# Transposing unit 4's x with the DMA crossbar in place of the tensor engine

## The chip, the core and the metric

The kernel runs on one core of one Trainium2 chip. The metric is device time in microseconds (us) of one execution, start to end; less is better. Engines are named as the profile names them: PE is the tensor engine and PEld its weight loads, DVE the vector engine, ACT the scalar engine, POOL and SP two further ones that issue DMAs. A DMA *lands* when its last data have arrived; times to landing are counted from its issue. A profiled execution also has a *span*, from its first to its last recorded instruction, and every timed run lists its span too. The time of the kernel before is 1.73 to 1.91 us longer than its span in all of its listed runs.

## The reference

Chunked attention (8 batches, 8 heads, 576 tokens, head size 64, chunks of 64), whose output, 4608 tokens by 512, goes through a two-layer network with a gated activation:

```python
scores = scale * q_c @ k_c.T                  # per chunk of 64
attn   = softmax(scores)
x      = (attn @ v_c)  ->  (B*S, H*D) = (4608, 512)
h = x @ w_in                                  # 512 -> 2048
g = h * (1 / (1 + exp(-beta * h)))
out = g @ w_out                               # 2048 -> 512
```

## The kernel before

The tokens are cut into 18 units of 256. Two units form a block of 512 tokens, on which the network runs. For each unit: the scores (`emit_sc`), the product with v (`emit_pv`), a division by the sum that leaves x in fp16 (`emit_norm`), and a transpose of x, since the first layer needs its features on the partitions. Each unit has two halves of 128 tokens. The transpose comes in two kinds:

```python
def emit_xt_pe(u, s, copy=nc.scalar.copy):          # on the tensor engine
    xf = x16_t.pop((u, s)).rearrange("p r h d -> p (r h d)")
    ...
    for g in range(4):
        nc.tensor.transpose(out=xp[:, g, :], in_=xf[:, g * 128:(g + 1) * 128], identity=ident)
    copy(out=xt_at(u, s), in_=xp)                   # PSUM -> SBUF, on ACT

def emit_xt_dma(u, s):                              # in the DMA crossbar
    xf = x16_t.pop((u, s)).rearrange("p r h d -> p (r h d)")
    nc.sync.dma_start_transpose(out=xt_at(u, s), in_=xf)
```

`emit_T` transposes a unit's keys and queries: on DVE (by blocks) for units below 8, by DMA from SP from unit 8 on. The network of block j is `emit_m(j, m)`, first layer, which reads the transposed x; and `emit_t(j, t, k0, k1)`, second layer, ending in an output DMA from SP. The second layer of one block is spread among the first layer of the next. The program order is written by hand; the part that matters:

```python
        emit_t(1, 0, 0, 8)
        emit_pv(4)
        emit_norm(4, 0)
        emit_norm(4, 1)
        emit_T(5)
        emit_T(6)
        emit_t(1, 0, 8)
        emit_xt_pe(4, 0)
        emit_xt_pe(4, 1)
        emit_t(1, 1, 0, 8)
        emit_sc(5)
        emit_t(1, 1, 8)
        ...                                   # unit 5 in the same way, on the tensor engine
        for m in range(KFF):                  # block 2 = units 4 and 5
            emit_m(2, m)
            ...                               # units 6 and 7: emit_norm, emit_xt_dma
        for j in range(3, NB):                # block 3 = units 6 and 7, and so on
            items = [(0.02 + 0.98 * m / KFF, 0, ("m", m)) for m in range(KFF)]
            for t in range(4):
                for hf in range(2):
                    items.append((0.98 * (t + 0.5 * hf) / 4, 1, ("t", t, hf)))
            ...                               # attention items of the next two units
            items.sort(key=lambda it: it[:2]) # so t(j-1, 0, first half) is ahead of m(j, 0)
```

So eight matmuls of the old block stand ahead of the new block's first matmul.

The softmax here doesn't subtract the row's maximum and nothing guards it: scores larger than these inputs give would overflow.

Of the kernel before, what the change touches and what calls it, by code (L numbers as in the profile page):

```python
# [15 lines left out]
def kernel(  # L16
# [108 lines left out]
    def loads_to(u):  # L125
        while nxt[0] <= min(u, NU - 1):
            load_unit(nxt[0])
            nxt[0] += 1
# [16 lines left out]
    def emit_T(u, which=("kT", "qT")):  # L145
        for nm in which:
            src, dst = {"kT": (k_t, kT), "qT": (q_t, qT)}[nm]
            a = src.pop(u)
            t = qt_p.tile([128, H, CH, 2], FP16, tag=nm, name=nm)
            dst[u] = t  # L150
            if u >= XU:
                nc.sync.dma_start_transpose(
                    out=t.rearrange("p h s e -> p (h s e)").rearrange("p (j t) -> p j t", t=128),
                    in_=a.rearrange("p h r d -> p (h r d)"),
                )
                continue
            nc.vector.transpose(
                out=t.rearrange("p h s e -> p (h s e)").bitcast(FP32).rearrange(
                    "p (h i r) -> p h r i", h=H, r=2),
                in_=a.rearrange("p h r d -> p (h r d)").bitcast(FP32).rearrange(  # L160
                    "p (h r i) -> p h r i", h=H, r=2),
            )
        if which[-1] == "qT" and u not in (6, 7, 8):
            loads_to(u + 4)
# [89 lines left out]
    def emit_pv(u, where=("x", "s")):  # L254
        et = et_t.pop(u)
        for s in (1, 0) if u >= MU else (0, 1):
            i = 2 * u + s
            if where[s] == "p":
                x = [ps_p.tile([128, 4, 128], FP32, tag="p", name=f"y{r}") for r in range(2)]
            else:  # L260
                pool = {"x": ps_x, "s": ps_s}[where[s]]
                x = [pool.tile([128, 2, 4, 128], FP32, tag=where[s], name="x")]
            for g in range(4):
                for r in range(2):
                    for c in range(2):
                        nc.tensor.matmul(  # L266
                            out=(x[0][64 * c:64 * c + 64, r, g, 0:D + 1] if len(x) == 1 else
                                 x[r][64 * c:64 * c + 64, g, 0:D + 1]),
                            lhsT=(et[64 * r:64 * r + 64, s, 4 * c + g, :] if u < XU else
                                  et[64 * r:64 * r + 64, g % 2, 4 * s + 2 * c + g // 2, :]),  # L270
                            rhs=vbig[64 * r:64 * r + 64, i, 4 * c + g, 0:D + 1],
                        )
            x_t[u, s] = x
# [6 lines left out]
    def emit_norm(u, s):  # L280
        x = x_t.pop((u, s))
        rd = rd_p.tile([128, 2, 4, 1], FP32, tag="rd", name="rd")
        x16 = x_p.tile([128, 2, 4, D], FP16, tag="x16", name="x16")
        for r, z in [(slice(0, 2), x[0])] if len(x) == 1 else list(enumerate(x)):
            nc.vector.reciprocal(out=rd[:, r], in_=z[..., D:D + 1])  # L285
            o = x16[:, r]
            nc.vector.tensor_tensor(  # L287
                out=o, in0=z[..., 0:D], in1=rd[:, r].to_broadcast(list(o.shape)), op=ALU.mult
            )
        x16_t[u, s] = x16  # L290

    def xt_at(u, s):
        j, o = unit_block[u]
        if j not in xt_t:
            xt_t[j] = xt_p.tile([128, 4, 4, 128], FP16, tag="xt", name="xt")
        return xt_t[j][:, 2 * o + s]

    def emit_xt_pe(u, s, copy=nc.scalar.copy):
        xf = x16_t.pop((u, s)).rearrange("p r h d -> p (r h d)")
        tag = "s" if u < 2 and (u, s) != (1, 0) else "xp"[s]  # L300
        xp = {"x": ps_x, "s": ps_s, "p": ps_p}[tag].tile([128, 4, 128], FP16, tag=tag, name="xp")
        for g in range(4):
            nc.tensor.transpose(out=xp[:, g, :], in_=xf[:, g * 128:(g + 1) * 128], identity=ident)  # L303
        copy(out=xt_at(u, s), in_=xp)  # L304
# [11 lines left out]
    def emit_xt_dma(u, s):  # L316
        xf = x16_t.pop((u, s)).rearrange("p r h d -> p (r h d)")
        nc.sync.dma_start_transpose(out=xt_at(u, s), in_=xf)
# [36 lines left out]
    def emit_t(j, t, k0=0, k1=None):  # L355
        k1 = KFF if k1 is None else k1
        if k0 == 0:
            ops_t[j, t] = ps_p.tile([128, DM], FP32, tag="p", name="ops")
        ops = ops_t[j, t]
        for kk in range(k0, k1):  # L360
            nc.tensor.matmul(  # L361
                out=ops,
                lhsT=gt_t[j][:, kk, t * 128:(t + 1) * 128],
                rhs=w_out16[kk // 4][:, kk % 4, :],
                start=(kk == 0),
                stop=(kk == KFF - 1),
            )
        if k1 < KFF:
            return
        osb = osb_p.tile([128, DM], FP32, tag="osb", name="osb")  # L370
        nc.scalar.activation(out=osb, in_=ops, func=ACTF.Copy, scale=0.5)  # L371
        r0 = blocks[j][0] * UNIT + t * 128
        nc.sync.dma_start(out=out[r0:r0 + 128, :], in_=osb)
# [20 lines left out]
    with tc.manual_schedule():  # L394
# [111 lines left out]
                emit_ex(4)  # L506
        emit_t(1, 0, 0, 8)
        emit_pv(4)
        emit_norm(4, 0)
        emit_norm(4, 1)  # L510
        emit_T(5)
        emit_T(6)
        emit_t(1, 0, 8)
        emit_xt_pe(4, 0)
        emit_xt_pe(4, 1)
        emit_t(1, 1, 0, 8)
        emit_sc(5)
        emit_t(1, 1, 8)
# [125 lines left out]
```

## Time and profile before

| | kernel before |
|---|---|
| time, first three runs | 288.05 us median (287.95 to 288.5) |
| profiled span | 286.6 us |
| tensor engine (PE) busy | 98% of the span, 96% of the chain of waits |
| PE waits after 58 us | none |
| transposes of x: on PE (four per half unit) / by crossbar (one per half unit) | 48 (40 at line 303, 8 at line 311) / 24 |

The view of groups: line, engine, operation, output from inputs, shape, count; then busy us, mean ns of one; then idle time before, by releaser.

```profile
L303 PE MATMUL xp<-ident,x 128*128 128x128 f16 x40 | 3.5, 219 | 0.1
```

The transposes of unit 7's x, asked for by their line between 90.2 and 92 us, of which the second, issued at 91.2, landed after 4.1 us, at 95.3:

```profile
DMA to landing us min/median/max: 4.1/4.4/4.7
```

And the waits of SP's queue in the last microseconds (us in total, times, longest): line 639 is the end of the program, where SP waits for outstanding DMAs.

```profile
SPq L639 <- DMA out_dram<-osb: 1.3, 3, 0.5
```

### The profile page before, as it was taken

What the parts mean: (1) busy time and instruction counts of PE and PEld (TensorE: products, weight loads), DVE (VectorE), ACT (ScalarE), POOL (GpSimd) and SP (SyncE); (2) the same over time, 40 slices, a digit from 0 to 9 for tenths busy, and PEclk for the clock granted to TensorE, in tenths of its full rate; (3) what the DMA queues carried; (4) which work ended last, traced back from release to release, by engine and by line L of the source; (5) the groups of instructions that cost most, each with busy time, mean ns of one, the idle gap of its engine ahead of it and who ended that gap; (6) DMA issues with size and microseconds to landing.
All of it is one profiled execution on the core that took longest, in us unless ns stands there. A gap on an engine that the chain in (4) does not pass through costs nothing.

```text
span 286.6 us, 6655 instructions
## 1 busy us (share of the span) xinstructions
PE 280.4 (98%) x2777; PEld 136.4 (48%) x2777; DVE 141.9 (49%) x260; ACT 147.0 (51%) x225; POOL 95.7 (33%) x125
## 2 busy tenths in 40 slices
PE   6989999999999999999999999999999999999995
PEld 3564456545544444444444444444444444444444
DVE  2778444776567544534454445454554545333300
ACT  3478228774557545454545454554545444444411
POOL 8853678487172992070907160000000000000000
PEclk9999999999999999999999999999999999999999
DMA  8999999999999999999999999565451212010012
GB/s 193 175 196 206 182 180 215 206 166 165 153 95 182 155 176 167 165 119 168 137 158 145 143 124 171 129 75 128 57 129 39 73 39 73 37 39 37 37 73 75
DMA packets 139997, 37.14 MB, mean 130 GB/s; under 512 B 126912, under 2 KB 135488, under 8 KB 139968
## 3 DMA queue, kind: packets, MB, share of 16 engines
q0 software_dynamic: 99136, 17.83, 82.4%
q1 hardware_dynamic: 40688, 18.83, 32.2%
q8 instruction: 22, 0.36, 0.5%
q14 instruction: 7, 0.06, 0.1%
q10 hardware_dynamic: 144, 0.07, 0.1%
HBM read 36.71 MB, written 9.44 MB: 161 GB/s over the span
## 4 chain that ended last, share of the span: by engine, by line
PE 96%; ACT 1%; POOL 1%; issue 1%; DVE 0%; DVEq 0%; POOLq 0%
PE hps L329 44%; PE ops L361 43%; PE warm L381 2%; PE x L266 2%; PE sc L238 1%; PE sc L225 1%; PE ops L600 1%; ACT xt L304 1%; PE xp L303 1%; POOL h L401 1%; PE sc L198 1%; POOL vbig L113 1%; ACT et L208 0%; PE y L266 0%; PE xp L311 0%
## 5 line engine op out<-in xcount | busy, mean ns | idle before, releaser
L343 DVE SCALAR_TENSOR_TENSOR gt<-sg,hps 128x512 f16<-128x512 f32 (+1 forms) x153 | 99.1, 654 | 107.4 <-ACT sg L339 107.2
L339 ACT ACTIVATE sg<-hps,beta 128x512 f32<-128x512 f32 (+1 forms) x153 | 100.4, 663 | 72.9 <-PE hps L329 72.8
L329 PE MATMUL hps<-xt,win 128*128 128x512 f16 (+1 forms) x612 | 136.8, 367 | 0.8 <-ACT xt L304 0.7
L361 PE MATMUL ops<-wout,gt 128*128 128x512 f16 x560 | 131.2, 379 | 0.0
L329 PEld LDWEIGHTS <-win 128*128 128x128 f16 x612 | 58.1, 98 | 62.1 <-issue 1.0
L361 PEld LDWEIGHTS <-gt 128*128 128x128 f16 x560 | 53.9, 98 | 63.4
L371 ACT ACTIVATE osb<-ops 128x512 f32<-128x512 f32 x35 | 20.9, 598 | 42.5 <-PE ops L361 42.5
L113 POOL DMA_DIRECT2D vbig<-in_v_dram x40 | 34.1, 871 | 9.6 <-DMA wout<-in_moe_w_out_dram 3.7
L99 POOL DMA_DIRECT2D qu<-in_q_dram x22 | 18.7, 863 | 40.1 <-DMA qT<-qu 37.1
L287 DVE TENSOR_TENSOR x<-x,rd 128x512 f16<-128x512 f32 x31 | 21.4, 691 | 1.2
L99 POOL DMA_DIRECT2D ku<-in_k_dram x22 | 18.9, 877 | 0.6 <-DMA ku<-in_k_dram 0.6
L285 DVE RECIPROCAL rd<-x 128x8 f32<-128x8 f32 x31 | 6.2, 200 | 12.0 <-PE x L266 12.0
L247 ACT ACTIVATE et<-sc 128x1024 f16<-128x1024 f32 (+1 forms) x8 | 6.4, 811 | 8.2 <-PE sc L238 8.2
L231 ACT ACTIVATE et<-sc 128x1024 f16<-128x1024 f32 x10 | 10.2, 1018 | 0.2
L266 PEld LDWEIGHTS <-et 64*64 64x64 f16 x576 | 6.0, 107 | 7.3 <-issue 3.8
L381 PE MATMUL warm<-idle 128*128 128x512 f16 x22 | 8.2, 518 | 0.0
L105 POOL DMA_DIRECT2D ku<-in_k_dram x9 | 6.8, 756 | 2.5 <-DMA win<-in_moe_w_in_dram 1.3
L266 PE MATMUL x<-vbig,et 64*64 64x65 f16 x496 | 7.3, 194 | 0.2 <-ACT et L208 0.2
L105 POOL DMA_DIRECT2D qu<-in_q_dram x9 | 6.8, 767 | 1.4 <-DMA win<-in_moe_w_in_dram 0.7
L612 DVE TENSOR_SCALAR osb<-ops 128x256 f32<-128x256 f32 (+1 forms) x2 | 0.7, 357 | 12.1 <-PE ops L600 12.1
L131 POOL DMA_DIRECT2D win<-in_moe_w_in_dram x8 | 6.0, 757 | 1.2 <-DMA vbig<-in_v_dram 0.9
L304 ACT COPY xt<-xp 128x512 f16<-128x512 f16 x9 | 5.1, 588 | 2.3 <-PE xp L303 2.2
(46 smaller groups left out, 73.4 us busy)
## 6 DMA issues: line engine op xcount, KB each, us to landing
out_dram<-osb SPq DMA_DIRECT2D x35, 256.0 KB, 3.7
vbig<-in_v_dram POOLq DMA_DIRECT2D x32, 128.0 KB, 7.6
qu<-in_q_dram POOLq DMA_DIRECT2D x20, 128.0 KB, 4.9
ku<-in_k_dram POOLq DMA_DIRECT2D x20, 128.0 KB, 6.8
win<-in_moe_w_in_dram POOLq DMA_DIRECT2D x8, 256.0 KB, 9.0
wout<-in_moe_w_out_dram POOLq DMA_DIRECT2D x4, 512.0 KB, 12.3
qu<-in_q_dram POOLq DMA_DIRECT2D x3, 256.0 KB, 7.7
ku<-in_k_dram POOLq DMA_DIRECT2D x3, 256.0 KB, 8.0
```

The source lines that it names most:

```text
L99: nc.gpsimd.dma_start(out=tv[off:off + n, sp], in_=src[b, :, s:s + n, :].rearrange("h p d -> p h d"),)
L105: nc.gpsimd.dma_start(out=t[off // 2:(off + n) // 2], in_=src[b, :, s:s + n, :].rearrange("h (p r) d -> p h r d", r=2),)
L113: nc.gpsimd.dma_start(out=vbig[off:off + n, i, :, 0:D], in_=v[b, :, s:s + n, :].rearrange("h p d -> p h d"),)
L231: nc.scalar.activation(out=et, in_=sc, func=ACTF.Exp, scale=scale)
L266: nc.tensor.matmul(out=(x[0][64 * c:64 * c + 64, r, g, 0:D + 1] if len(x) == 1 else x[r][64 * c:64 * c + 64, g, 0:D + 1]), lhsT=(et[64 * r ...
L287: nc.vector.tensor_tensor(out=o, in0=z[..., 0:D], in1=rd[:, r].to_broadcast(list(o.shape)), op=ALU.mult)
L329: nc.tensor.matmul(out=hps[:, 0:n], lhsT=w_in16[m // 2][:, kk, (m % 2) * 128:(m % 2) * 128 + 128], rhs=xr[:, c0 // CH:(c0 + n) // CH, 2 * ...
L339: nc.scalar.activation(out=sg[:, 0:n], in_=hps[:, 0:n], func=ACTF.Tanh, scale=beta2[:, m:m + 1])
L343: nc.vector.scalar_tensor_tensor(out=gt_t[j][:, m, c0:c0 + n], in0=sg[:, 0:n], scalar=1.0, in1=hps[:, 0:n], op0=ALU.add, op1=ALU.mult,)
L361: nc.tensor.matmul(out=ops, lhsT=gt_t[j][:, kk, t * 128:(t + 1) * 128], rhs=w_out16[kk // 4][:, kk % 4, :], start=(kk == 0), stop=(kk == K ...
L371: nc.scalar.activation(out=osb, in_=ops, func=ACTF.Copy, scale=0.5)
L381: nc.tensor.matmul(out=d[:, 0:w], lhsT=idle[:, 0:128], rhs=idle[:, 0:w])
```

## The change

The intent is to relieve the tensor engine, which sets the time: its transposes of unit 4's x go to the crossbar. The second half is normalized first so that its transfer starts early, and unit 5's block transposes on DVE run between the two norms. Unit 5's x stays on the tensor engine.

```diff
         emit_t(1, 0, 0, 8)
         emit_pv(4)
+        emit_norm(4, 1)
+        emit_xt_dma(4, 1)
+        emit_T(5)
         emit_norm(4, 0)
-        emit_norm(4, 1)
-        emit_T(5)
+        emit_xt_dma(4, 0)
         emit_T(6)
         emit_t(1, 0, 8)
-        emit_xt_pe(4, 0)
-        emit_xt_pe(4, 1)
         emit_t(1, 1, 0, 8)
```

## The prediction

> **What bounds the kernel now.** I read the page first: busy shares, the 40 slices, the chain that ended last.
>
> ```profile
> PE 280.4 (98%) x2777; PEld 136.4 (48%) x2777; DVE 141.9 (49%) x260; ACT 147.0 (51%) x225; POOL 95.7 (33%) x125
> ...
> PE   6989999999999999999999999999999999999995
> ...
> DMA  8999999999999999999999999565451212010012
> ...
> PE 96%; ACT 1%; POOL 1%; issue 1%; DVE 0%; DVEq 0%; POOLq 0%
> ```
>
> The tensor engine is busy in every slice after the first few, and 96% of the chain is its own work. The other compute engines are about half idle, so their time is worth something only where PE waits for it. The DMA engines are full until about slice 26 (near 186 us), so a transfer added early has to share.
>
> The chain of waits, cut to the stretch where the change lies (start us, us, what):
>
> ```profile
> 63.91 0.38 PE x L266 x32
> 64.29 1.83 PE ops L361 x8
> 66.12 0.45 PE xp L303 x8
> 66.57 1.73 PE ops L361 x8
> 68.30 0.64 PE sc L238 x64
> 68.94 1.83 PE ops L361 x8
> 70.77 0.38 PE x L266 x32
> 71.14 1.83 PE ops L361 x8
> 72.98 0.45 PE xp L303 x8
> 73.42 0.64 PE sc L238 x64
> 74.06 1.83 PE ops L361 x8
> 75.90 0.86 PE hps L329 x4
> ```
>
> Each start is the previous start plus its length: nothing on PE waits here. The `xp` piece at 66.12 is the eight transposes that the change removes; the one at 72.98 is unit 5's and stays. The view of waits, asked for PE between 58 and 100 us, lists none at all; the PE waits of the whole run (at most 1.2 us each) lie before that.
>
> **What the Trainium skill says.** "TensorE: Matmul & The Clock Gate", Part 4, says a PE transpose ends in PSUM, so a copy has to follow, and puts one at about 275 ns in a kernel's context. Here one record lasts 219 ns, but they are pipelined: eight take 0.45 us of the chain, 56 ns each, and I use that. "Advanced Engine Details and Errata", X-Bar Transpose, says transposing DMAs are as fast as regular ones. The trace agrees when the engines are idle: 128 x 512 fp16 (128 KB) landed 2.5 us after issue at 79.1 us. "DMA: Bandwidth & Descriptors", Queues, rings and completion order, says each DMA engine goes round the queues packet by packet, so a transpose is not stuck behind the whole load backlog but shares with it. The trace agrees in kind: outputs on the hardware queue landed in 3.7 and 5.2 us in the crowded 66 to 77 us. The same page, Silent corruption, warns of two transposing streams; all transposes here are issued from SP, one stream, so I expect a correct result.
>
> **The change, part by part.**
>
> Removed from PE: eight transposes and their weight loads, 0.45 us of the chain. What follows them is the same 8-matmul group; in the list it takes 1.73 us after a transpose and after another full matmul group, 1.83 us only after the small attention matmuls. After the change its predecessor is a full matmul group, so it stays at 1.73. Net on PE: -0.45 us.
>
> Removed from ACT: two PSUM copies, 1.07 us together. ACT then reaches exp(5) with no copies ahead. But PE did not wait for that exp: pv(5) came at 70.70 and exp had ended at 69.00 + 1.02 = 70.02, behind eight covering matmuls. Worth 0.
>
> Removed from PSUM: one use of each of two pools. The next users wait for an older tile instead of a newer one; looser, and no wait was there. Worth 0.
>
> Moved on DVE: the same eight instructions in another order. From the timeline one norm takes about 0.93 us and one pair of block transposes about 1.3. The tiles of pv(4) are complete at 64.29, so norm(4,1) runs 64.3 to 65.2, unit 5's block transposes to 66.5, norm(4,0) to 67.4, unit 6's to 68.7. sc(5) will be reached at 68.30 - 0.45 = 67.85. Its keys and queries are ready at 66.5 (before: about 67.2), and its PSUM slot, read last by norm(4,1), is free at 65.2. pv(5) at about 70.3 needs the slot freed by norm(4,0) at 67.4. No new wait.
>
> Added on SP: two transposes, about 1.2 us of issue each, the first at about 65.3, the second at about 67.4. The first output of block 1 sits behind them in the same queue, so it goes out near 68.7 instead of 66.78: 1.9 us late. The instruction order shows the output buffer's next user four outputs later, so nobody should notice.
>
> Added to the DMA engines: two transposes beside the loads of units 8 and 9. The windows view (PE and so on, last three: clock, DMA share, GB/s):
>
> ```profile
> 64.00:66.00 2.00, 2.00 (x41) 1.01 (x34) 1.71 (x5) 0.00 (x0) 1.99 (x3) 1.00 2.39 152
> 66.00:68.00 2.00, 2.00 (x17) 1.09 (x15) 2.00 (x4) 1.56 (x3) 0.50 (x1) 1.00 2.39 156
> ...
> 76.00:78.00 2.00, 2.00 (x41) 0.94 (x40) 0.48 (x1) 1.22 (x2) 0.00 (x0) 1.00 0.68 138
> ...
> 79.00:81.00 2.00, 2.00 (x11) 0.92 (x10) 1.45 (x4) 0.27 (x1) 0.40 (x2) 1.00 0.31 62
> ...
> 106.00:108.00 2.00, 2.00 (x11) 0.90 (x10) 1.82 (x4) 0.79 (x3) 2.00 (x4) 1.00 2.44 152
> ```
>
> At 65 to 68 us the share is 2.39 (packets outstanding, so over 1). The stretch most like it is 106 to 108, at 2.44, and there the two transposes took 7.2 and 7.0 us to land, the longest of all:
>
> ```profile
> L318 SPq DMA_TRANSPOSE xt<-x x24: 1189/1196/1902, 79.1 to 237.5; - x24
> ...
> DMA to landing us min/median/max: 2.4/2.9/7.2
> ```
>
> So I take 7.2 us, not the median: landings at 72.5 and 74.6. The first reader is the weight load of block 2's first matmul, at 75.52 before, so 75.1 after. It gained waits for the two transposes, by the instruction order. Slack 0.5 us at the longest landing seen, 4.8 us at the median. Each transpose alone keeps the engines full for some 0.8 us (the slices at 80.3 to 81.1), so the loads of unit 9 end perhaps 1.6 us later than their 76.5; the engines then stand nearly empty until 80.4, and unit 9's keys are wanted first at 92.6. Hidden. Its loads also start 0.7 us earlier, as unit 5's queries are released earlier.
>
> Sum: -0.45 + 0 + 0 + 0 = -0.45 us, 288.05 to 287.6, or 0.16%.
>
> **The rivals.**
>
> 1. The transposes land late and PE waits at block 2's first matmul. For it: the crowd, the 0.5 us slack at the longest landing, and that the kernel elsewhere holds the loads of units 10 and 11 back behind a gate until the norms of units 6 and 7 are done, as if this had hurt once; the change has no such gate. Against: the queues share packet by packet, and after 105 us a second pair for keys and queries competed as well, which it doesn't here. With the longest landing of any transpose in the trace, 10.5 us for a queries tile of twice the size, the second would land at 77.9 and PE would wait 2.8 us: 290.4, 0.8% slower. About 1 in 8 for any wait, most of it under 1 us.
>
> 2. The 0.45 us comes back later: PE arrives earlier at something that goes by the load queue's pace. For it: the DMA engines are full to 186 us. Against: the later loads are gated by norm(6,1) and norm(7,1) or by released buffers, so they move forward with PE; the tightest case I found, block 3's first matmul, has its transpose issued at 91.2, landing after 4.1 us at 95.3, and is reached at 96.4. Time then 288.0. About 1 in 8.
>
> 3. It gains more, because ACT and DVE are relieved and PSUM rotates more freely. No PE wait exists there to be shortened, so at most 0.1 us more. About 1 in 10: 287.4.
>
> **Range and chances.** The three runs before spread from 287.95 to 288.5, as wide as the effect. I put 287.6, with 0.4 below for noise and rival 3, and 0.7 above for noise, rival 2 and the small end of rival 1: 287.2 to 288.3. Two per cent is 5.8 us; the removed work totals 0.45 on PE, so faster by that is out of reach (0.01). Slower by it would take a wait twice that of rival 1's worst case (0.01). Within 2%: 0.98.
>
> **What would show each step.** In the chain after, the matmul groups at 64.29 and 66.12 follow each other without `xp`, and sc(5) starts near 67.85. The matmul transpose group loses eight and the ACT copy two. The added pair lands 4 to 7 us after issue. The PE waits between 58 and 100 us stay empty; a line there from block 2's first matmul, or its weight load, to the transposed x proves rival 1. If each later block starts 0.45 us earlier and the end too, the sum is right; if the lead shrinks between 80 and 190 us, rival 2. I'd be wrong outright if the block transposes of unit 5 came later and sc(5) waited for DVE.

## More of the kernel before

The chain of waits where block 3 begins (start us, us, what): the first first-layer matmuls start at 96.60, right behind the eight of the old block.

```profile
94.87 1.73 PE ops L361 x8
96.60 0.86 PE hps L329 x4
```

## The result, and the profile after

| | before | after |
|---|---|---|
| median of six runs | 288.36 us (287.95 to 289.33) | 289.04 us (288.66 to 289.73) |
| profiled span | 286.6 us | 286.8 us |
| ratio after / before | | 1.0025, 95% interval 1.0003 to 1.0046 |

A ratio is the mean time of one kernel's fast runs over that of the other's in the same rounds, so it is not quite the ratio of the medians. The change did not gain the predicted 0.45 us: it lost about 0.7. Its median also lies above the predicted range. Of the 1.44 us between 287.6 and 289.04, 0.31 is the kernel before, which itself had a median of 288.36 in these rounds; the rest is the change.

The page of the changed kernel: eight matmuls fewer, PE still the chain.

```profile
PE 280.1 (98%) x2769; PEld 135.9 (47%) x2769; DVE 141.9 (49%) x260; ACT 146.0 (51%) x223; POOL 95.6 (33%) x125
...
PE 95%; ACT 1%; POOL 1%; issue 1%; DVE 0%; DVEq 0%; POOLq 0%
```

The groups and, in the next fence, the chain where the change lies. The transposes of line 303 went from 40 to 32, and the matmuls of block 1's second layer, which were two groups with `xp` between them, now form one group of 16. Scores of unit 5 start at 67.83 (67.85 was predicted), and block 2 at 75.43, 0.47 us earlier than the 75.90 of before.

```profile
L303 PE MATMUL xp<-ident,x 128*128 128x128 f16 x32 | 2.9, 219 | 0.1
```

```profile
64.27 3.56 PE ops L361 x16
67.83 0.64 PE sc L238 x64
...
75.43 0.86 PE hps L329 x4
```

The two added transposes, asked for by their line between 64 and 70 us: issued at 65.3 and 67.3, landed 6.3 and 5.6 us later, in time for block 2.

```profile
L318 SPq DMA_TRANSPOSE xt<-x x2: 1291/1372/1452, 65.3 to 67.3; - x2
...
DMA to landing us min/median/max: 5.6/5.9/6.3
```

The windows view (stretch; busy of PE, PEld, DVE, ACT, POOL; clock, DMA share, GB/s). At 76 to 78 us the DMA engines moved 138 GB/s at a share of 0.68 before; now:

```profile
76.00:78.00 2.00, 2.00 (x41) 1.03 (x40) 0.91 (x3) 1.07 (x3) 0.00 (x0) 1.00 2.02 230
```

By the records of the two traces the last load of unit 9 landed at 78.87 in place of 78.24, 0.6 us later; at 78 to 80 us the DMA engines are nearly idle again (share 0.19). Then, at block 3, the chain of waits after:

```profile
94.41 1.73 PE ops L361 x8
96.14 0.10 issue
96.24 1.02 PE hps L329 x4
```

PE came 0.46 us earlier than before (94.41 against 94.87); this is called its lead below. It stood for 0.10 us, and its first four matmuls then took 1.02 us in place of 0.86. Of the 0.46, 0.26 is gone, and 0.20 is left (97.26 against 97.46 at the end of the four). The second half of unit 7's x is why: issued at 90.8, it took 5.2 us and landed at 96.0. The view of waits of the weight loads shows the same place, with the releaser not named:

```profile
DMA to landing us min/median/max: 5.2/5.6/5.9
```

```profile
PEld L329 <- issue: 0.6, 1, 0.6
```

The lead of 0.2 us stays to the end: the last group of 48 matmuls starts at 279.94, against 280.13. Yet the program ends later. The view of SP's waits at the end:

```profile
SPq L639 <- DMA out_dram<-osb: 2.1, 2, 1.2
```

Two waits in place of three, the longest 1.2 us in place of 0.5. The reason is seen in the trace's own records of SP's instructions, which no view lists. They are given here as start times (us) of SP's successive waits on DMA semaphores (the counters that tell of a DMA's landing), then of the drain that follows:

```
before  ... 284.20  284.26  284.74  285.15  285.71                                   drain 285.77
after           283.34  284.54  285.51  285.57  285.64  285.70  285.76  285.82  285.88   drain 285.94
```

SP goes through a fixed list of semaphores, 0.06 us each. The instruction stream shows the hardware queue's DMAs taking eight semaphores in turn. Before, the last output's semaphore stands at the end of the list. Two DMAs more turn the rotation by two places, the last output's semaphore is now earlier in the list, and six waits, each long satisfied, come after it. The last landing itself is 0.20 us earlier (285.51 against 285.71), and the drain is 0.17 later: 0.37 us more.

In this traced pair the account closes: 0.02 from the start and 0.44 from the transposes gained, 0.26 given back at block 3, 0.37 lost at the end, net +0.17, and the spans are 286.8 against 286.6.

### The profile page after: what moved, and what is told of

Its sections match the earlier page's. It is cut to its first block, busy times and chain, and to the rows that moved or that the text cites. A ratio compares the mean times of both kernels' runs of the same rounds, so it can differ in the third digit from the quotient of the medians.

```text
span 286.8 us, 6644 instructions
## 1 busy us (share of the span) xinstructions
PE 280.1 (98%) x2769; PEld 135.9 (47%) x2769; DVE 141.9 (49%) x260; ACT 146.0 (51%) x223; POOL 95.6 (33%) x125
## 4 chain that ended last, share of the span: by engine, by line
PE 95%; ACT 1%; POOL 1%; issue 1%; DVE 0%; DVEq 0%; POOLq 0%
PE hps L329 44%; PE ops L361 43%; PE warm L381 2%; PE x L266 2%; PE sc L238 1%; PE sc L225 1%; PE ops L600 1%; ACT xt L304 1%; POOL h L401 1%; PE sc L198 1%; POOL vbig L113 1%; PE xp L303 0%; ACT et L208 0%; PE y L266 0%; PE xp L311 0%
## 5 line engine op out<-in xcount | busy, mean ns | idle before, releaser
L157 DVE STREAM_TRANSPOSE kT<-ku 128x512 f32<-128x512 f32 x6 | 4.2, 707 | 4.0 <-DMA ku<-in_k_dram 4.0
```

## The experiments

Spans are means over the runs, on the same chip within each set. "Second landing" is that of the transpose of unit 7's second half.

| run | what it is | ratio to before (95%) | mean span, it / before |
|---|---|---|---|
| `e1_again` | the changed kernel, unedited | 1.0018 (0.9994 to 1.0041) | 287.05 / 286.69 |
| `e2_order` | before, new DVE order alone | 1.0035 (1.0021 to 1.0048) | 287.72 / 286.69 |
| `e3_drop` | unit 4's transposes dropped | 0.9999 (0.9979 to 1.0018) | 286.27 / 286.69 |
| `e4_slack` | after, slack before block 3 (flawed) | 1.0199 (1.0176 to 1.0222) | 292.32 / 286.69 |
| `e5_relief` | after, slack before blocks 3 and later | 0.9993 (0.9974 to 1.0011) | 286.92 / 287.08 |
| `e6_relief_before` | before, the same slack | 0.9995 (0.9980 to 1.0010) | 286.88 / 287.08 |
| `e7_traffic` | before, four spare transposes | 1.0000 (0.9985 to 1.0014) | 287.10 / 287.08 |
| `e8_drop_two` | transposes of units 4 and 5 dropped | 0.9965 (0.9949 to 0.9980) | 286.10 / 287.08 |
| `e9_filler` | after, PE's gained time filled | 1.0039 (1.0017 to 1.0060) | 287.82 / 286.79 |
| `e10_old_order` | after, old DVE order | 1.0024 (1.0002 to 1.0046) | 287.37 / 286.79 |
| `e11_again` | the changed kernel, unedited | 1.0019 (1.0005 to 1.0033) | 287.28 / 286.79 |
| `e13_two_pads` | before, two small late DMAs | 1.0037 (1.0015 to 1.0060) | 287.77 / 286.64 |
| `e14_six_pads` | after, six small late DMAs | 1.0017 (0.9999 to 1.0034) | 286.87 / 286.64 |
| `e15_relief_pads` | after, slack and six DMAs | 1.0000 (0.9980 to 1.0019) | 286.25 / 286.64 |
| `e16_null` | before against itself | 0.9999 (0.9986 to 1.0013) | 286.67 / 286.64 |
| `e17_two_pads_in_place` | before, two DMAs into old tiles | 1.0005 (0.9991 to 1.0018) | 286.88 / 286.77 |
| `e18_relief_pads_in_place` | after, slack and six DMAs into old tiles | 1.0001 (0.9988 to 1.0013) | 286.66 / 286.77 |

The theory at the start was that the added transfers crowd the DMA engines and the loss is taken at block 3's first matmul. The rivals: the DVE order costs something; PE's work was never worth its 0.45 us; PE merely comes too early at block 3 whatever the transfers do.

### The changed kernel again: `e1_again`, `e11_again`, `e12_again`

No edit.

> The changed kernel once more, unedited. Crowding theory (the added transposes delay later landings until block 3's first matmul waits): the trace shows a wait of 0.1 to 1 us there, near 96 us, and the ratio to the kernel before lies between 0.999 and 1.004, different from run to run. Noise theory (the removed 0.45 us is really saved and the first timing was unlucky): ratio 0.998 to 0.9995.

> The changed kernel again, to see how often it waits. Theory of thin slack with luck in it: single spans spread over more than 1.5 us (the kernel before: about 1 us), some at 286, some above 287.5; the traced run either has 230.1 us between the two marks of the chain and no wait, or more than 230.3 and a wait for transposed x at the first matmul of block 3, 4 or 5. If the first timing was bad luck: mean span 0.3 to 0.5 us below the kernel before's.

> One more look at the changed kernel for its trace: between the two marks of the chain 230.1 us if nothing waits, more with a wait at a block's first matmul (blocks 3 to 5) otherwise.

Measured: 1.0018 and 1.0019, with mean spans 0.36 and 0.49 us above the kernel before; with the first 1.0025, three comparisons give a loss of 0.5 to 0.7 us (the interval of `e1_again` alone includes no loss). The executions differ. In the trace of `e1_again` the second landing took 4.0 us and nothing waited at block 3; in `e11_again` 5.0 us, and 0.01 us was lost. The one of `e12_again` lost 0.91; its chain and its waits:

```profile
90.78 5.87 DMA xt<-x
96.65 0.25 issue
96.90 1.02 PE hps L329 x4
```

```profile
PE hps L329 <- DMA xt<-x: 0.8, 1, 0.8
```

Here the releaser is named. The chain runs through the transfer: issued at 90.78, 5.87 us to landing, 0.25 us more to the matmul. All four traces of the unedited kernel (the first result's and these) have 0.43 us from the last landing to the drain. That last landing itself came 1.62 us after its issue in two of them and in the kernel before, 1.87 and 2.08 us in the other two. What follows: the wait at block 3 is real, by execution 0.26, 0, 0.01 and 0.91 us, about 0.3 on average.

### The order on DVE: `e2_order` and `e10_old_order`

```diff
 # e2_order, against before
         emit_pv(4)
-        emit_norm(4, 0)
         emit_norm(4, 1)
         emit_T(5)
+        emit_norm(4, 0)
         emit_T(6)
```

> The kernel before with the new order of the vector engine alone (second half normalized, unit 5's block transposes, first half, unit 6's); the x of unit 4 still goes through the tensor engine. Unit 9's loads then start 0.7 us earlier. Crowding theory: no added transfer, so the same as before, ratio 0.999 to 1.001, no wait at block 3's first matmul. Order theory (the earlier loads or the later first half cost the time): ratio 1.0015 to 1.004, as the changed kernel.

Measured: 1.0035, slower. But this edit makes its own wait, because it leaves the tensor engine's transposes of the first half in place, and these now wait for a norm that comes later:

```profile
PE xp L303 <- DVE x L287: 1.3, 1, 1.3
```

The changed kernel has no such transposes, so this run says nothing of it. It was a flawed test; the clean one goes the other way, from the changed kernel:

```diff
 # e10_old_order, against after
         emit_pv(4)
+        emit_norm(4, 0)
+        emit_xt_dma(4, 0)
         emit_norm(4, 1)
         emit_xt_dma(4, 1)
         emit_T(5)
-        emit_norm(4, 0)
-        emit_xt_dma(4, 0)
         emit_T(6)
```

> The changed kernel with the vector engine's old order: both halves normalized and sent to the transposing DMA first, then the block transposes of units 5 and 6. The second transpose goes out about 0.7 us sooner, unit 9's loads start 0.7 us later. If the order brings the loss: ratio 0.998 to 0.9995 and 230.1 us in that stretch of the chain. If lead and traffic bring it: as the changed kernel, 0.9995 to 1.003, 230.1 to 231 us.

Measured: 1.0024, as slow as the changed kernel, with the wait at block 3:

```profile
91.22 6.04 DMA xt<-x
```

```profile
PE hps L329 <- DMA xt<-x: 0.9, 1, 0.9
```

The order of the DVE work is not the cause.

### Is PE's work worth its time? `e3_drop`, `e8_drop_two`, `e9_filler`

The first two compute a wrong result (relative error 0.239 and 0.334): x of the unit is set to zero in place of being transposed, so there is neither PE work nor transfer.

```diff
 # e3_drop, against before; e8_drop_two does the same for unit 5 as well
+        for s in range(2):
+            x16_t.pop((4, s))
+            nc.vector.memset(xt_at(4, s), 0.0)
         emit_t(1, 0, 8)
-        emit_xt_pe(4, 0)
-        emit_xt_pe(4, 1)
```

(The lines stand between `emit_T(6)` and `emit_t(1, 1, 0, 8)`.)

> The kernel before with unit 4's eight transposes and two copies taken out and nothing in their place (its transposed x is filled with zeros by two vector memsets: a wrong result on purpose, for the rows of unit 4). If 0.45 us of tensor work is really on the path: 0.4 to 0.5 us faster, ratio 0.998 to 0.999, and the last matmuls 0.45 us earlier in the trace. If the lead is eaten later even without the added transfers: ratio 1.000 and a wait near 96 us.

> The kernel before with the transposes and copies of units 4 and 5 both taken out, no transfers added (zeros in their place, wrong on purpose for those rows): a lead of 0.9 us on the tensor engine. If the engine's own work sets the time: ratio 0.9965 to 0.9975. Early-arrival theory (the lead is eaten by waits for landings that do not move with the engine): ratio 0.999 to 1.001, with a wait in the trace between 96 and 160 us of up to 0.9 us.

Measured: `e3_drop` left the time unchanged (0.9999), though its spans fell by 0.42 us; the time outside the span rose to a mean of 2.24 us, from 1.79, in these runs. Its traced execution also lost half a microsecond at block 4, behind an output transfer:

```profile
PE hps L329 <- DMA out_dram<-osb: 0.5, 1, 0.5
```

Taken alone it spoke for the rival that PE's work isn't worth its time. `e8_drop_two` answers: twice the work gone, spans shorter by 0.98 us, time by 0.35%, no wait anywhere. The chain of waits shows both `xp` pieces gone, with block 2 starting at 75.26:

```profile
68.11 0.64 PE sc L238 x64
...
72.79 0.64 PE sc L238 x64
73.43 1.83 PE ops L361 x8
75.26 0.86 PE hps L329 x4
```

So each unit's transposes are worth some 0.45 to 0.5 us on the path, as predicted, if nothing takes their place. And a lead twice as large without the added transfers brings no wait at block 3, so coming early isn't enough by itself to lose the time; the section on `e7_traffic` shows why.

`e9_filler` puts matmuls that do nothing in the place of the transposes, to take away PE's lead and keep the transfers:

```diff
 # against after
         emit_t(1, 0, 8)
+        emit_idle(2, 512)
         emit_t(1, 1, 0, 8)
```

> The changed kernel with two idle 512-wide matmuls (about 0.43 us) at the place of the removed transposes, so that the tensor engine has no lead while transfers and vector order are the changed ones. If traffic or order cost time by themselves: ratio 1.001 to 1.004 and waits for transposed x near 96 us. If only lead and traffic together do: same as before, ratio 0.9995 to 1.001. In the chain, from the start of the 60-matmul stretch at about 49 us to the start of the last 48-matmul group: 230.5 us without waits, as before.

Measured: 1.0039, spans 1.03 us above before, 0.54 more than `e11_again` in the same set. The expectation if only lead and traffic together cost time, 0.9995 to 1.001, was missed. Its trace has the end of 0.43 us, and at block 3 a second landing of 5.0 us with 0.07 us lost, though PE had no lead:

```profile
95.30 1.73 PE ops L361 x8
97.03 0.93 PE hps L329 x4
```

Its last landing took 3.26 us after issue in place of 1.62, which is no part of the change and explains much of that execution alone. With the lead gone the time rose by about the lead; the loss of the changed kernel is therefore not the lead handed back.

### Slack ahead of block 3: `e4_slack`, `e5_relief`, `e6_relief_before`

`e4_slack` moves the second eight matmuls of the old block's first tile ahead of block 3's first matmul, so that PE reaches it 1.73 us later at no cost of work.

```diff
 # e4_slack, against after
-                    items.append((0.98 * (t + 0.5 * hf) / 4, 1, ("t", t, hf)))
+                    items.append((0.01 if (j, t, hf) == (3, 0, 1) else 0.98 * (t + 0.5 * hf) / 4, 1, ("t", t, hf)))
```

> The changed kernel, with the second half of block 2's first output tile (8 matmuls, 1.73 us) put ahead of block 3's first matmul, so that the first reader of unit 7's transposed x comes 1.73 us later. Crowding theory with this as the only place: the wait near 96 us is gone, the last matmul is 0.45 us earlier than before's, ratio 0.998 to 0.999. If the loss sits elsewhere, or in the end of the program: ratio stays at 1.001 to 1.004.

Measured: 1.0199, six microseconds slower; the edit was flawed. With the matmuls their output DMA moved too, ahead of unit 9's key and query transposes in SP's queue, and SP worked that queue in order: by its timeline it stood at the output from 92.0 to 98.5 us, until the output was ready, and everything behind it was late. The view of waits:

```profile
PE sc L225 <- DMA qT<-qu: 1.9, 1, 1.9
PE hps L329 <- DMA xt<-x: 1.4, 2, 0.7
```

This is worth keeping as a fact, but it tests nothing. `e5_relief` mends it, by moving the key and query transposes forward as well, so that SP's order stays, and gives the slack to every block from 3 on; `e6_relief_before` is the same edit on the kernel before, as the control.

```diff
 # e5_relief against after, e6_relief_before against before
-                    (a0 + 0.10 * w, 3, ("T", u + 1))]
+                    (0.005 if a0 < 0.1 else a0 + 0.10 * w, 3, ("T", u + 1))]
 ...
-                    items.append((0.98 * (t + 0.5 * hf) / 4, 1, ("t", t, hf)))
+                    items.append((0.01 if (t, hf) == (0, 1) else 0.98 * (t + 0.5 * hf) / 4, 1, ("t", t, hf)))
```

> The changed kernel with every block's first matmul (from block 3 on) put behind the second half of the previous block's first output tile as well, so that the newest transposed x is wanted 1.73 us later; unlike the fourth experiment the transposes of keys and queries are emitted ahead of that output, so the SP queue keeps its order. Theory of thin slack at the blocks' first matmuls: those waits go, the saved 0.45 us arrives at the end, ratio 0.997 to 0.999. If the loss is elsewhere (end of the program, other waits): ratio 1.001 to 1.003 as the changed kernel.

> The kernel before with the same reordering. Its traced run had 1.3 us of slack or more at blocks 3 to 5, so thin-slack theory: little to win, ratio 0.999 to 1.0005, and the fifth experiment beats it by about 0.45 us. If the reordering itself costs or gains something, it shows here and is to be taken off the fifth experiment.

Measured: 0.9993 and 0.9995. The relief does nothing measurable to the kernel before, and brings the changed kernel from 1.0018 or more to below 1.0. In its chain block 3 starts at 98.18, behind 16 matmuls in place of 8:

```profile
94.73 3.45 PE ops L361 x16
98.18 0.86 PE hps L329 x4
```

Each interval overlaps with that of the unedited kernel. But all five comparisons of the changed path without relief lie between 1.0017 and 1.0025 (the first result, `e1_again`, `e10_old_order`, `e11_again`, `e14_six_pads`), and all three with relief between 0.9993 and 1.0001 (`e5_relief`, `e15_relief_pads`, `e18_relief_pads_in_place`). As far as sets on different chips can be compared, the loss goes with the reach of block 3 or a later block.

### The transfers without the lead: `e7_traffic`

Four crossbar transposes of unit 4's x into spare tiles that nobody reads, in the kernel before: twice the added traffic, and PE's work as it was.

```diff
 # against before
         emit_norm(4, 1)
+        for i in range(4):
+            spare = const.tile([128, 4, 128], FP16, name=f"spare{i}")
+            nc.sync.dma_start_transpose(
+                out=spare, in_=x16_t[4, i % 2].rearrange("p r h d -> p (r h d)"))
         emit_T(5)
```

> The kernel before, its tensor work untouched, with four spare transposing DMAs of unit 4's x at the place where the change puts two: twice the change's traffic alone. Crowding theory (the added transfers push later landings): slower, ratio 1.001 to 1.005, with waits for transposed x at blocks 3 to 5. Early-arrival theory (only the tensor engine's lead eats the slack, traffic is harmless): ratio 0.9995 to 1.001 and no new wait.

Measured: 1.0000. The second landing took 5.1 us, the weight load waited, and the first four matmuls took 0.94 us in place of 0.86:

```profile
DMA to landing us min/median/max: 5.1/5.1/5.1
```

```profile
PEld L329 <- issue: 0.4, 1, 0.4
```

```profile
95.21 1.73 PE ops L361 x8
96.93 0.94 PE hps L329 x4
```

So the added transfers alone, with no lead, already bring the late landing. In time it cost nothing that this comparison could see; but its half-width is 0.4 us, and the end of this kernel (next section, 0.25 us) doesn't show in it either.

Why the lead doesn't matter at block 3 can be read from the records of the traces. Unit 7's second half is transposed as soon as DVE has normalized it, and DVE gets it from PE's own products with v; so the issue moves with PE (91.24 before, 90.78 after). From this issue until PE is due at block 3's first matmul, 1.73 us after the start of the old block's eight, 5.20 to 5.21 us pass in every one of the fifteen traces with eight matmuls there, with a lead or without. Where PE then had to stand, the first matmul came 0.25 us after the landing (0.14 in `e7_traffic`). That leaves 4.95 us for the landing, and what it takes beyond is lost:

| traces | second landing, us (lost at block 3, us) |
|---|---|
| no added transfer | before 4.08, `e16_null` 4.43, `e2_order` 4.17, `e3_drop` 4.34, `e6_relief_before` 4.21, `e8_drop_two` 4.87, `e13_two_pads` 4.60, `e17_two_pads_in_place` 4.16 (none lost) |
| added transfers | `e1_again` 4.01 (0), `e11_again` 4.96 (0.01), `e9_filler` 5.03 (0.07), `e7_traffic` 5.14 (0.08), after 5.22 (0.26), `e14_six_pads` 5.82 (0.86), `e12_again` 5.87 (0.91), `e10_old_order` 6.04 (1.09) |
| added transfers, 16 matmuls ahead, due after 6.92 us | `e4_slack` 4.73, `e5_relief` 5.04, `e15_relief_pads` 5.13, `e18_relief_pads_in_place` 4.95 (none lost) |

Ten of the twelve landings with added transfers are longer than 4.87 us, the longest of the eight without. The two kernels with a lead but no added transfer had 4.34 and 4.87; the two with added transfers but no lead 5.03 and 5.14. So the longer landing goes with the added transfers and not with the lead. How two transfers at 65 to 73 us lengthen a landing at 91 to 97 us isn't shown: in the changed kernel the DMA engines were nearly idle in between, at 78 to 80 us. Nor is the amount of traffic told apart from the number of DMAs on the queue up to there, which `e7_traffic` and the change both raise, and which the pads, coming later, do not.

### The end of the program: `e13_two_pads` to `e18_relief_pads_in_place`

If the number of DMAs on the hardware queue turns the rotation, two tiny DMAs late in the kernel before should bring the 0.37 us, and six more in the changed kernel (two and six make eight) should take it away.

```diff
 # e13_two_pads: against before, range(2).  e14_six_pads: against after, range(6).
 # e15_relief_pads: e14_six_pads and the edit of e5_relief
             emit_t(NB - 1, t)   # the last loop ahead of the final groups
+        for i in range(2):
+            pad = const.tile([128, 16], FP16, name=f"pad{i}")
+            nc.sync.dma_start(out=pad, in_=idle[:, 0:16])
```

> The kernel before with two tiny DMAs (4 KB within the chip, read by nobody) put into the SP queue late, when the DMA engines are nearly empty, and nothing else. End-of-program theory: the last landing is followed by six waits, 0.43 us to the drain in place of 0.06, so 0.37 us slower, ratio 1.001 to 1.002, and 230.5 us between the marks of the chain as before. If the number of DMAs does not matter: 0.9995 to 1.0007.

> The changed kernel with six such tiny DMAs, so that eight are added in all and the last outputs fall on the same semaphores as in the kernel before. 0.06 us from the last landing to the drain. Ratio to before: 0.9985 to 0.9995 if only the end ate the gain, 0.9995 to 1.002 if the waits at block 3 eat it too, which I expect (0.3 us on average).

> The changed kernel with the six tiny DMAs and the later first matmul of each block (the fifth experiment's edit). Both losses are away: 230.1 to 230.2 us between the marks, 0.06 us at the end, ratio 0.998 to 0.9995. Should it not be below 1, a third loss is left.

> The kernel before, unedited, against itself: ratio 0.9985 to 1.0015 by chance alone; 230.5 us between the marks, no wait at block 3, 0.06 us at the end.

Measured, from the records of SP's last waits (waits after the last landing; us from it to the drain):

```
before 0, 0.06      e16_null 0, 0.06     e8_drop_two 0, 0.06     (no DMA added)
after  6, 0.43      e13_two_pads 6, 0.43                         (two added)
e7_traffic 4, 0.31                                               (four added)
e14_six_pads 0, 0.06      e15_relief_pads 0, 0.06                (eight added)
```

The mechanism is shown: the end depends on the number of DMAs modulo eight. Every traced kernel obeys it but for one small deviation, told below. What it is worth in time is less clear. `e13_two_pads` lost 1.0037, almost three times 0.37 us; its traced execution reached the long matmul stretch 1.4 us later than the kernel before and waited once where that one doesn't, at block 5:

```profile
PE hps L329 <- issue: 0.6, 1, 0.6
```

Its pads were new tiles, two of 32 bytes per partition, which can move the addresses of the tiles after them, so the run is confounded. `e14_six_pads` restored the end and still has the wait at block 3 in its trace, so the two causes are separate, but its time (1.0017) did not fall below that of the unedited kernel:

```profile
PE hps L329 <- DMA xt<-x: 0.7, 1, 0.7
```

`e15_relief_pads`, with both mended, has mean spans 0.39 us below before, nearly the 0.44 that both repairs should leave; its time is 1.0000 all the same, as its time outside the span rose to 2.39 us from 1.80. The null run gives 0.9999, with half-width 0.0014, so differences under 0.4 us are not seen by one such comparison.

The last two were to remove the confounding: the pads go into tiles that exist and are no longer read.

```diff
 # e17_two_pads_in_place: against before, range(2)
 # e18_relief_pads_in_place: against after, range(6), with the edit of e5_relief
+        for i in range(2):
+            nc.sync.dma_start(out=late if i == 4 else tiny[:, 16 * (i % 5):16 * (i % 5) + 16] if i < 4
+                              else braw[:, 0:8].bitcast(FP16), in_=idle[:, 0:16])
```

> The kernel before with two tiny DMAs late in the SP queue, written into tiles that exist already, so that no address moves. End-of-program theory alone: 0.43 us from the last landing to the drain, mean span 0.3 to 0.5 us longer than the kernel before's, ratio 1.0008 to 1.002. If the number of DMAs does more than that: 1.0025 to 1.005 as in the thirteenth run.

> The changed kernel with the later first matmul of each block and six tiny DMAs into existing tiles: 230.1 to 230.2 us between the marks, 0.06 us at the end, mean span 0.3 to 0.6 us shorter than the kernel before's, ratio 0.998 to 0.9995. A ratio of 1 with such spans would mean that something outside the span takes it back, as in the fifteenth run.

Measured: 1.0005 and 1.0001. `e17_two_pads_in_place` shows the six waits and 0.43 us, and mean spans 0.11 us above before; 0.37 us would be a ratio of 1.0013, inside its interval, as is zero. So the extra loss of `e13_two_pads` is not owed to the number of DMAs; its addresses or chance are left, and that is open. `e18_relief_pads_in_place` drains 0.13 us after the last landing, with one wait after it, because the last landing was not that of the last DMA in this execution; spans 0.11 us below before, time the same. No version that computes the right result was clearly faster than both kernels.

## Why the prediction was wrong

**What held.** The removed work was worth what was said: `xp` left the chain, scores began at 67.83 (67.85 predicted), block 2 at 75.43 (0.47 us earlier), and `e8_drop_two` shows two such units to be worth 0.98 us of span. DVE's order, ACT's copies and PSUM cost nothing, with no PE wait between 58 and 96 us. Rival 1, a wait at block 2's first matmul, didn't come: the pair landed 5.6 and 6.3 us after issue, within the 7.2 allowed.

**The step that failed first: "Hidden", the cost of the two transfers for what lands after them.** The prediction followed them to the loads of unit 9 and found these wanted late enough. There it erred on the safe side: it has these loads ending at 76.5 us and 1.6 later after the change; by the records the last landed at 78.24, and 0.6 later. But at the place that rival 2 named, block 3's first matmul, it held the landing at the 4.1 us of one trace and left out the 0.25 us from landing to matmul. With the change the landing there took 4.0 to 6.0 us where 4.95 is allowed, which lost 0 to 0.91 us by execution, 0.3 on average in the four unedited traces; more than the lead was worth in one of them. Rival 2's own mechanism, PE coming earlier at something that doesn't move with it, isn't what happened: the issue moved with PE, as the prediction's "against" said of the loads, and the allowance stayed at 4.95 us. The relief, which takes this wait away and adds no gain to the kernel before, is the only repair that moved the time (1.0017 to 1.0025 without it, 0.9993 to 1.0001 with it).

**The step that was missing: the end of the program.** The sum had no term for the two DMAs more. In every trace of the unedited kernel they put six satisfied waits, 0.37 us, after the last landing. This is shown in the traces; its worth in total time was not resolved by the runs that undid or made it.

**The sum, corrected** (us against before): -0.44 PE, +0.37 end, about +0.3 at block 3, and about +0.2 outside the span (means 2.10, 1.97 and 1.87 in the three comparisons, against 1.8 before): about +0.4. Measured: +0.5 to +0.7, with intervals of some 0.4 to 0.7 either way. Later last landings, 1.87 and 2.08 us in two of the four traces, may hold a part of the rest.

**What stays open.** The time outside the span rises in some kernels (the changed one, `e3_drop`, `e14_six_pads`, `e15_relief_pads`) and not in others, `e5_relief` among them, and no record shows why. The spans of the changed kernel also scatter more, 286.2 to 288.9 in the unedited runs, and only one execution of each set was traced, so the average wait at block 3 rests on four traces. And the way from the added transfers to the longer landings at block 3 isn't known.

## What to carry to other kernels

Moving work off the engine that sets the time is worth its time only as far as no transfer makes that engine wait: at the next places where it meets one, take the time from the transfer's issue to its use, and see whether the issue moves with the engine (here it did, so the lead cost no slack) or not. Allow the landing to grow to the longest seen under the same load, and add the time from landing to use. A transfer added elsewhere can lengthen it. Where the slack is short, put covering work that needs nothing new ahead of the first use, without moving a DMA in an in-order queue ahead of those that others wait for. For effects of tenths of a microsecond, look at the last waits of the program too: adding DMAs can change the end, and a null run tells what a comparison can show at all.

## What the Trainium skill lacked or had wrong

- No page that I read has the end of the program seen here: SP waits for eight DMA semaphores in a fixed order, 0.06 us each, the DMAs of the hardware queue take them in turn, and so two DMAs more made the drain come 0.43 us after the last landing in place of 0.06, four 0.31, eight 0.06.
- "Advanced Engine Details and Errata", X-Bar Transpose, compares transposes with regular DMAs but says nothing of landing under load: here the same 128 x 512 fp16 transpose landed 2.4 us after issue on idle engines and 4.0 to 6.0 us at one and the same place of eleven executions that carry the change, against 4.1 to 4.9 us in eight without added transfers.
- "TensorE: Matmul & The Clock Gate", Part 4, gives about 275 ns for a transpose (bf16) in a kernel's context; here (fp16) one record is 219 ns and eight pipelined ones take 0.45 us of the chain, 56 ns each, and removing sixteen shortened the spans by 0.98 us, 61 ns each.
